# Dense and dilated-window attention with a gated sum: half the input by transposing DMAs, bound and query read-out re-ordered, planner settings changed

## The chip, the cores and the metric

The kernel runs on one core of a Trainium2 chip. The metric is device microseconds of one execution; the median of three runs before the change is 895.62 us (894.89 to 896.11).

The core has five engines with a queue of their own: TensorE (PE, matmuls; its weight loads are listed as PEld), VectorE (DVE), ScalarE (ACT), GpSimd (POOL) and SyncE (SP, here only a queue of DMAs). ACT and POOL issue DMAs too. Engines wait for each other by semaphores, and each works through its own list in order.

## The reference

Two attentions over the same input x (2048 x 640, bfloat16), with 32 heads of width 20, are mixed by a gate for each row.

```python
g = sigmoid((x * gate_w).sum(-1, keepdims=True))
# A: dense attention
q, k, v = split(x @ A_wqkv)             # (32 heads, 2048, 20)
p = softmax(q @ k.T * 20 ** -0.5)       # 2048 x 2048 for each head
a = merge(p @ v) @ A_wo
# B: eight keys for each row, at distance 0, 2, ..., 14 behind it
logits = where(idx >= 0, (q_B * k_B[idx]).sum(-1) * 20 ** -0.5, -1e9)
b = merge((softmax(logits)[..., None] * v_B[idx]).sum(w)) @ B_wo
out = g * a + (1 - g) * b
```

## The kernel before, in words

**Tiles.** The 32 heads of A are taken in eight quads of four; each head of a quad has 32 partitions (one for a bias, 20 for values), so that a quad fills 128. Queries are taken in four chunks of 512. A group is one chunk of one quad: 16 key blocks of 128 times four heads, 64 score units of 128 x 512. There are 32 groups and 2048 units. `GO` (line 37) is the order of the groups. Before, chunks 0 and 1 alternate for quads 0 to 3, then chunk 0 takes quads 4 to 7, then chunk 1; chunks 2 and 3 follow, all quads each.

**A step.** `mk_qk` (line 1233) puts the scores of three or two units into PSUM banks, in turns (banks 0 to 2, banks 3 and 4); `mk_exp` (line 1253, the instruction on line 1256) reads them with one exponential on ACT into one of six buffers `ebuf`. `mk_pv` (line 1267) multiplies the buffers with the values and sums in bank 5. When a group is closed, `gen_norm` (line 707) transposes, divides by the sum and multiplies by the gate on DVE.

**The bound.** Instead of a row's maximum, a bound on it is subtracted: the keys' largest absolute value in each channel (`k_max`, line 482, four pieces for a quad, and `mk_KM`, line 487) times the queries' absolute values (`q_abs`, `q_fin`, lines 658 to 668). One matmul adds the negative bound to a spare row of the projected query in its bank, and DVE reads the bank out as `qT`.

**Exponentials on DVE.** Some units go to DVE instead of ACT: `gen_xm` (line 1355) takes a free bank (6 or 7) or, by `xstep` (line 1331), the third bank of a step, and has the score matmul done; `gen_x` (line 1406) computes two units as a pair, in integer and polynomial steps, on lines 1424 to 1448. `X0` is the first step at which a unit may start, `XMIN` and `XLAST` are how many units a group (the last group) must have left, and 64 - `XAHEAD` is that number for the group after the current one.

**The planner.** The whole order is worked out when the kernel is built. Each piece of other work is a lane, a generator that says on which engine its next instruction runs and for how long. The main loop (line 1785) keeps a clock for each engine; before each step it fills PE's time until the step's banks come free with value matmuls, lanes, and spare matmuls (`spare`, line 1706, which write nothing that is read and run only while PE's share of work is under `SPW`). The lanes are: `gen_v`, `gen_k`, `gen_q` (projections of A), `gen_late` (weights of B and the output weights), `gen_F` (projections and logits of B for one chunk), `gen_K` (values, softmax and weighted sum of B), `gen_fold` (output projection of a chunk) and `gen_prefold` (the last chunk's in part). Their starts are steps (`gstep`, `FSTART`), and k, v and q lanes have due steps (`open_group`, line 1588). While a due step is less than six steps away, no new DVE unit starts (`urgent`, line 1298); `behind` and `hot` hold units back too, the first by a pace for the DVE work of the lanes (`LW`, `LS`). `GRP` is the least size of a batch of value matmuls.

**The start.** Lines 383 to 395 issue the loads: the first K weights on ACT's queue; x in eight tiles of 256 rows, the Q weights, the gate vector and the V weights on SP's. `pro_tr` (line 1103) transposes a tile by ten PE transposes, read out by DVE and ACT; `pro_k` (line 1127) projects the keys of quad 0 for it, DVE takes the largest value and ACT reads the keys out; `pro_q` (line 1147) projects the first query group in two halves. Lines 1163 to 1202 set their order by hand: a transpose, then the K projection of the tile before it. The bound, one group of values (read out by ACT) and `q_fin` close the start; then the main loop begins.

SP's queue carries, after that, the head weights of A (`ld_w`, line 434, five DMAs with runs of 40 bytes each), B's weights in blocks of 160 KB (`ldw`, line 884, in `gen_F`; three buffers) and the stores.

## Time and profile before

| | |
|---|---|
| median of three runs | 895.62 us |
| the profiled execution | 894.33 us, span 892.5 us |
| first exponential starts | 18.18 us |
| exponentials on ACT | 777, 1902 units |
| units on DVE | 146 |
| last exponential ends | 883.17 us |
| granted TensorE clock | 0.999 |

How to read it: times are from the start of the span, which is 1.8 us shorter than the execution's own time. A row names line, engine, operation, the tile written and the tiles read, shapes, count, busy time, mean duration, and the idle time of the engine just before, with the instruction that ended it. "ps" is PSUM. Instructions on one engine overlap a little, so that their mean duration is more than the distance from start to start. The DMA queue of an engine is its name with a q. Rows of x take 1280 bytes, the B weight blocks have rows of 256 bytes.

### The profile page before, as it was taken

What the parts mean: (1) busy time and instruction counts of PE and PEld (TensorE: products, weight loads), DVE (VectorE), ACT (ScalarE), POOL (GpSimd) and SP (SyncE); (2) the same over time, 40 slices, a digit from 0 to 9 for tenths busy, and PEclk for the clock granted to TensorE, in tenths of its full rate; (3) what the DMA queues carried; (4) which work ended last, traced back from release to release, by engine and by line L of the source; (5) the groups of instructions that cost most, each with busy time, mean ns of one, the idle gap of its engine ahead of it and who ended that gap; (6) DMA issues with size and microseconds to landing.
All of it is one profiled execution on the core that took longest, in us unless ns stands there. A gap on an engine that the chain in (4) does not pass through costs nothing.

```text
span 892.5 us, 15877 instructions
## 1 busy us (share of the span) xinstructions
PE 820.1 (92%) x6560; PEld 255.5 (29%) x6560; DVE 811.9 (91%) x1170; ACT 876.2 (98%) x804; POOL 87.8 (10%) x103
## 2 busy tenths in 40 slices
PE   9989999999999998999998889999988999888986
PEld 6322322223323222223332222233222232222322
DVE  6598889999998999999899999999999899999994
ACT  6999999999999999999999999999999999999996
POOL 1000000000000011220002222001322002222000
PEclk9999999999999999999999999999999999999999
DMA  8122101011011456572115658113847003865000
GB/s 181 41 49 48 21 9 10 1 28 7 4 11 14 86 93 94 90 123 37 17 19 88 111 102 145 25 16 56 143 78 108 10 10 74 131 93 89 2 1 30
DMA packets 140988, 51.26 MB, mean 57 GB/s; under 512 B 120436, under 2 KB 128628, under 8 KB 140916
## 3 DMA queue, kind: packets, MB, share of 16 engines
q0 software_dynamic: 13824, 31.46, 20.5%
q1 hardware_dynamic: 126164, 18.35, 13.4%
q8 instruction: 52, 0.85, 0.4%
q10 hardware_dynamic: 928, 0.43, 0.2%
q14 instruction: 20, 0.16, 0.1%
HBM read 16.14 MB, written 2.62 MB: 21 GB/s over the span
## 4 chain that ended last, share of the span: by engine, by line
ACT 94%; PE 2%; DMA 2%; DVE 1%; issue 0%; POOL 0%; DVEq 0%
ACT ebuf L1256 93%; DMA accW<-tmps 1%; PE ps L1112 1%; DMA accW<-xT 1%; PE ps L1136 1%; ACT L_sb L1004 0%; PE ps L411 0%; PE ps L1241 0%; DVE tmps L1069 0%; DVE accW L1059 0%; DVE qk L905 0%; ACT WvB L841 0%; PE ps L565 0%; DVE xH L1436 0%; PE ps L1153 0%
## 5 line engine op out<-in xcount | busy, mean ns | idle before, releaser
L1256 ACT ACTIVATE ebuf<-ps 128x1024 bf16<-128x1024 f32 (+1 forms) x777 | 862.7, 1485 | 0.9 <-PE ps L1241 0.8
L1241 PE MATMUL ps<-qT,kT 32*128 32x512 bf16 x1941 | 305.6, 384 | 63.9 <-ACT ebuf L1256 55.1
L1281 PE MATMUL ps<-ebuf,vA 128*21 128x512 bf16 x1902 | 182.6, 383 | 0.5 <-ACT ebuf L1256 0.5
L1241 PEld LDWEIGHTS ps<-qT,kT 32*128 32x128 bf16 x1941 | 74.3, 91 | 351.7 <-ACT ebuf L1256 327.2
L1424 DVE TENSOR_SCALAR xI<-ps 128x512 int32<-128x512 f32 x146 | 99.4, 686 | 28.3 <-PE ps L1396 14.8
L1436 DVE SCALAR_TENSOR_TENSOR xH<-xU 128x1024 f32<-128x1024 f32 x73 | 88.9, 1218 | 1.4
L1071 POOL DMA_DIRECT2D accW<-tmps x36 | 32.0, 987 | 586.2 <-DVE tmps L1069 545.8
L1439 DVE SCALAR_TENSOR_TENSOR xH<-xH,xU 128x1024 f32<-128x1024 f32 x73 | 88.7, 1216 | 1.0
L1448 DVE SCALAR_TENSOR_TENSOR xo<-xI,xH 128x1024 int16<-128x1024 int32 x73 | 88.7, 1215 | 0.6
L463 PE MATMUL ps<-xT,WqkB 128*128 128x512 bf16 x200 | 59.9, 383 | 0.0
L1281 PEld LDWEIGHTS ps<-ebuf,vA 128*21 128x21 bf16 x1902 | 35.8, 90 | 64.6 <-issue 56.7
L942 DVE TENSOR_TENSOR prod<-qk 128x1024 bf16<-128x1024 bf16 x80 | 51.8, 681 | 0.3 <-PE ps L918 0.3
L1433 DVE TENSOR_SCALAR xU<-xI 128x1024 f32<-128x1024 uint16 x73 | 49.8, 682 | 0.6
L463 PE MATMUL ps<-xT,WqP 128*128 128x512 bf16 x155 | 46.7, 383 | 0.0
L463 PE MATMUL ps<-woA_r,oTn 128*128 128x320 bf16 x236 | 45.3, 301 | 0.0
L463 PE MATMUL ps<-xT,accW 128*128 128x512 bf16 x140 | 42.2, 383 | 0.0
L1717 PE MATMUL ps<-ident,zt 128*128 128x512 bf16 x119 | 40.8, 386 | 0.0
L1712 PE MATMUL ps<-xT,ident 128*128 128x512 bf16 x130 | 40.1, 384 | 0.6 <-DVE qk L905 0.6
L1396 PE MATMUL ps<-qT,kT 32*128 32x512 bf16 x107 | 38.9, 383 | 0.8 <-DVE kT L475 0.7
L1069 DVE TENSOR_TENSOR tmps<-vB,attnT 128x1280 f32<-128x1280 bf16 x24 | 35.5, 1478 | 1.4 <-DMA accW<-tmps 1.4
L1069 DVE TENSOR_TENSOR xT<-vB,attnT 128x1280 f32<-128x1280 bf16 x24 | 35.4, 1477 | 0.3 <-DMA xT<-xT 0.3
L463 PE MATMUL ps<-WvA,oBacc 128*128 128x320 bf16 x160 | 33.2, 302 | 0.1
(122 smaller groups left out, 730.1 us busy)
## 6 DMA issues: line engine op xcount, KB each, us to landing
accW<-tmps POOLq DMA_DIRECT2D x36, 320.0 KB, 4.2
accW<-xT POOLq DMA_DIRECT2D x24, 320.0 KB, 4.0
xT<-xT POOLq DMA_DIRECT2D x24, 320.0 KB, 4.6
WqkB<-in_B_wqkv_dram SPq DMA_DIRECT2D x40, 160.0 KB
xT<-tmps POOLq DMA_DIRECT2D x12, 320.0 KB, 3.8
WqP<-in_A_wqkv_dram SPq DMA_DIRECT2D x135, 20.0 KB
x_tm<-in_A_x_dram SPq DMA_DIRECT2D x8, 320.0 KB
out_dram<-outsb SPq DMA_DIRECT2D x24, 80.0 KB
```

The source lines that it names most:

```text
L463: ins = e.matmul(o, l, r, start=(k0 + k == 0), stop=(k0 + k == n - 1))
L942: t = T("dve", lambda e, r=r, q_ap=q_ap, k_ap=k_ap: e.tensor_tensor(prod[r][:, :, :], q_ap, k_ap, ALU.mult), reads=["qB", "kB"], writes=[( ...
L1069: T("dve", lambda e, vv=vv, av=av, m=m: e.tensor_tensor(tmp4[m], vv, av, ALU.mult), reads=["aT", "vB4"], writes=[("tmps", m)] + dead, cost ...
L1241: ins = e.matmul(bank[b0 + i], kT[32 * j:32 * j + 32, q, kb * P:(kb + 1) * P], qT[gi % NQT][32 * j:32 * j + 32, :], start=True, stop=True)
L1256: return T("act", lambda e: e.activation(ebuf[s % NEB][:, 0:512 * n], ps[:, b0 * 512:(b0 + n) * 512], ACTF.Exp, scale=LN2 / ONE), reads=[( ...
L1281: ins = e.matmul(bank[OB][32 * j:32 * j + DH + 1, :], vA[:, q, kb, VW * j:VW * j + DH + 1], ap, start=st, stop=sp)
L1424: r = T("dve", lambda e, b=b, i=i: e.tensor_scalar(xI[:, 512 * i:512 * i + 512].bitcast(I32), bank[b], XB, 0.0, op0=ALU.add, op1=ALU.max), ...
L1433: T("dve", lambda e: e.tensor_scalar(xU[:, :], xI[:, :].bitcast(U16)[:, 0:2048:2], XV[0], XV[1], op0=ALU.mult, op1=ALU.add), reads=[("xI", ...
L1436: T("dve", lambda e: e.scalar_tensor_tensor(xH[:, :], xU[:, :], XC[0], xU[:, :], ALU.add, ALU.mult), reads=["xU"], writes=["xH"], cost=1220)
L1439: T("dve", lambda e: e.scalar_tensor_tensor(xH[:, :], xH[:, :], XC[1], xU[:, :], ALU.add, ALU.mult), reads=["xU"], writes=["xH"], cost=1220)
L1448: t = T("dve", lambda e, r=r: e.scalar_tensor_tensor(xo[r][:, :].bitcast(I16), xI[:, :].bitcast(I32), XC[2], xH[:, :], ALU.mult, ALU.add), ...
L1717: T("pe", lambda e: e.matmul(bank[OB], zt[:, :], ones4, start=False, stop=False, skip_group_check=True), reads=["ident", "zt"], accum=[("o ...
```

## The change

The first four x tiles are loaded plainly, on ACT's queue, followed by the Q weights; the other four are written straight into `xT` by four transposing DMAs on SP's queue, from which the first Q weights are gone. Four tiles then need no PE transposes and no read-outs; their K projections wait for the DMA. The order of the start is written anew: a plain tile's transpose, its K projection and that of a transposed tile in turn; the query's two halves come before the last K projection, and the first group of values goes to the lane `gen_v` in the stream, where DVE reads it out.

`k_max` reads two key blocks of 512 at once. `q_fin` is two functions, and in `gen_q` the read-out is a step of its own that waits its turn on DVE. The memsets of `woA_r` go from DVE to POOL, and no longer wait two steps each. In `gen_F` the additional wait before a weight block (`told`) is gone. `GO` takes chunks in turns for quads 0 and 1 only. The rest are the planner's settings: starts, due steps, pace, the smallest batch, limits on units and on taking a bank, the place of the unit lane among the others, and PE's share up to which spare matmuls run. With `XI` = 0 its two new lines do nothing.

```diff
--- before.py
+++ after.py
@@ -34,7 +34,7 @@
 
-GO = [(c, q) for q in range(4) for c in range(2)] + [(c, q) for c in range(2) for q in range(4, NQUAD)] + [(c, q) for c in range(2, QCN) for q in range(NQUAD)]
+GO = [(c, q) for q in range(2) for c in range(2)] + [(c, q) for c in range(2) for q in range(2, NQUAD)] + [(c, q) for c in range(2, QCN) for q in range(NQUAD)]
 GI = {x: i for i, x in enumerate(GO)}
@@ -381,11 +381,13 @@
     T("act", lambda e: e.dma_start(WqkA[:, :, 80:160], wA_v[:, :, D:D + 80]), writes=[("WkA", 0)], dma=True)
-    for h in range(NH):
-        T("sp", lambda e, h=h: e.dma_start(x_tm[:, 2 * h:2 * h + 2, :], x_v[:, 2 * h:2 * h + 2, :]),
+    for h in range(4):
+        T("act", lambda e, h=h: e.dma_start(x_tm[:, 2 * h:2 * h + 2, :], x_v[:, 2 * h:2 * h + 2, :]),
           writes=[("x_tm", h)], dma=True)
-
-    T("sp", lambda e: e.dma_start(WqkA[:, :, 0:80], wA_v[:, :, 0:80]), writes=[("WqA", 0)], dma=True)
+    for h in range(4, NH):
+        T("sp", lambda e, h=h: e.dma_start_transpose(xT[:, h // 2, :, 256 * (h % 2):256 * (h % 2) + 256], A_x[0][256 * h:256 * h + 256, :]),
+          writes=[("xTt", h, 0)], dma=True)
+    T("act", lambda e: e.dma_start(WqkA[:, :, 0:80], wA_v[:, :, 0:80]), writes=[("WqA", 0)], dma=True)
 
@@ -479,16 +481,20 @@
 
+    KMC = 2
+
     def k_max(q, tcc):
-        T("dve", lambda e: e.tensor_reduce(Kmax[:, q % 2, tcc:tcc + 1], kT[:, q, tcc * 512:(tcc + 1) * 512], AX.X, ALU.max,
+        n = KMC
+        o = 4 if n == 4 else tcc // n
+        T("dve", lambda e: e.tensor_reduce(Kmax[:, q % 2, o:o + 1], kT[:, q, (tcc + 1 - n) * 512:(tcc + 1) * 512], AX.X, ALU.max,
                                            apply_absolute_value=True),
-          reads=[("kT", q, tcc)], writes=[("Kmax", q % 2, tcc)], cost=690)
+          reads=[("kT", q, tcc - i) for i in range(n)], writes=[("Kmax", q % 2, o)], cost=150.0 + 533.0 * n)
 
...
         if part == 0:
-            src = Kmax0[:, :] if q == 0 else Kmax[:, q % 2, 0:4]
+            src = Kmax0[:, :] if q == 0 else Kmax[:, q % 2, 0:4 // KMC]
             T("dve", lambda e: e.tensor_reduce(Kmax[:, q % 2, 4:5], src, AX.X, ALU.max),
-              reads=[("Kmax0", h) for h in range(NH)] if q == 0 else [("Kmax", q % 2, t) for t in range(4)],
+              reads=[("Kmax0", h) for h in range(NH)] if q == 0 else [("Kmax", q % 2, t) for t in range(4 // KMC)],
               writes=[("Kmax", q % 2, 4)], cost=160)
@@ -508,7 +514,7 @@
             free = [b for b in (6, 7) if not held[b]]
-            if free and (len(free) == 2 or forcing[0] or not xwant() or cur[0] is xl_[0]) and not (cur[0] is xl_[0] and not forcing[0] and clk["dve"] > clk["pe"] + 3000.0):
+            if free and (len(free) == 2 or forcing[0] or not xwant() or cur[0] is xl_[0]) and not (cur[0] is xl_[0] and not forcing[0] and clk["dve"] > clk["pe"] + 300.0):
                 b = min(free, key=lambda k: (only is not None and k != only, free_at[k]))
@@ -631,9 +637,10 @@
             give(b, k_evac(b, q, tcc))
-            yield ("dve", 690.0, 0.0)
-            k_max(q, tcc)
-        for part in (0, 1):
+            if tcc % KMC == KMC - 1:
+                yield ("dve", 150.0 + 533.0 * KMC, 0.0)
+                k_max(q, tcc)
+        for part in (0, 1) if KMC < 4 else (1,):
             yield ("dve", 300.0, 0.0)
@@ -651,7 +658,9 @@
         yield ("pe", MM, 1.0)
-        give(b, q_fin(b, gi, q))
+        q_bound(b, gi, q)
+        yield ("dve", 690.0, 0.0)
+        give(b, q_evac(b, gi))
 
@@ -661,8 +670,14 @@
     def q_fin(b, gi, q):
+        q_bound(b, gi, q)
+        return q_evac(b, gi)
+
+    def q_bound(b, gi, q):
         T("pe", lambda e: e.matmul(bank[b], KM[:, q, :], qabs_hi, start=False, stop=True, skip_group_check=True),
           reads=["qabs", ("KM", q)], accum=[("bk", b)], cost=MM)
+
+    def q_evac(b, gi):
         qmade.add(gi)
@@ -682,9 +697,7 @@
         for q in range(NQUAD):
-            yield ("dve", 330.0, 0.0)
-            T("dve", lambda e, q=q: e.memset(woA_r[:, q, :], 0.0), writes=[("woA_r", q, j) for j in range(4)], cost=330)
-            yield ("s", 2)
+            T("pool", lambda e, q=q: e.memset(woA_r[:, q, :].bitcast(FP32), 0.0), writes=[("woA_r", q, j) for j in range(4)], cost=900)
         for q in range(NQUAD):
@@ -879,7 +892,6 @@
         wld = {}
-        told = {}
 
@@ -894,11 +906,10 @@
                 ldw(wi + NWB - 1)
-                yield ("t", max(wld[wi][1].fin, told.get(wi, 0.0)))
+                yield after(wld[wi][1])
                 b = yield from take(True)
...
                 mms = [(bank[b], W[:, c, :], xT[:, tc, c, :]) for c in range(CN)]
-                told[wi + NWB - 1] = max(clk["sp"], clk["pe"]) + 5800.0
                 yield from chain(b, mms, [("WqkB", wld[wi][0]), ("xT", tc)])
@@ -1028,7 +1039,7 @@
 
-            T("pe", pe_tb, reads=["L", "ident"], writes=[("bk", b)], cost=700, mode="t")
+            T("pe", pe_tb, reads=["L", "ident"], writes=[("bk", b)], cost=700, mode="t", flow=430.0)
 
@@ -1124,9 +1135,11 @@
 
+    KO = (0, 4, 1, 5, 2, 6, 3, 7)
+
     def pro_k(h):
         t, o = divmod(h, 2)
-        b = 6 + o if h < NH - 1 else 1
+        b = 6 + KO.index(h) % 2 if h < NH - 1 else 1
         ap = bank[b][:, 0:256]
@@ -1136,7 +1149,7 @@
 
-        T("pe", fn, reads=w_keys("WkP", 0) + [("xTt", h, k) for k in range(2)], writes=[("bk", b)], cost=550)
+        T("pe", fn, reads=w_keys("WkP", 0) + [("xTt", h, k) for k in range(2 if h < 4 else 1)], writes=[("bk", b)], cost=550)
         r = T("dve", lambda e: e.tensor_reduce(Kmax0[:, h:h + 1], ap, AX.X, ALU.max, apply_absolute_value=True),
@@ -1161,37 +1174,32 @@
     pro_tr(0)
+    pro_k(0)
+    pro_k(4)
     pro_tr(1)
-    pro_k(0)
+    pro_k(1)
+    pro_k(5)
     pro_tr(2)
-    pro_k(1)
+    ld_wk(1)
+    ld_wq(1)
     pro_tr(3)
-    for h in range(4, NH - 1):
-        pro_k(h - 2)
-        pro_tr(h)
-        if h == 4:
-            ld_wk(1)
-            ld_wq(1)
-    pro_tr(NH - 1)
-    for h in range(NH - 3, NH):
-        pro_k(h)
-        if h == NH - 3:
-            mk_q0()
+    pro_k(2)
+    pro_k(6)
+    mk_q0()
+    pro_k(3)
+    pro_q(0)
+    pro_q(1)
+    pro_k(7)
     mk_KM(0, 0)
     mk_KM(0, 1)
-    pro_q(0)
+    q_fin(QB0, 0, 0)
     T("dve", lambda e: e.tensor_copy(WvA[:, :, 1:2], gw[:, :].rearrange("p (c k) -> p c k", k=1)), reads=["gw", "WvA"],
       writes=["WvA"], cost=170)
-    pro_q(1)
     ld_wk(2)
...
     for t in range(QCN):
-        sch.bufs[("xT", t)] = [sch.bufs[("xTt", 2 * t + 1, 1)][0], []]
-    for i_ in range(3):
-        v_chunk(3, 0, 0, i_, i_)
-    v_evac(3, 0, 0, "act")
-    q_fin(QB0, 0, 0)
+        sch.bufs[("xT", t)] = [sch.bufs[("xTt", 2 * t + 1, 1 if t < 2 else 0)][0], []]
 
@@ -1310,10 +1318,10 @@
 
-    XAHEAD = 20
+    XAHEAD = 36
     XMIN = 28
-    X0 = 25
-    XLAST = 20
+    X0 = 18
+    XLAST = 16
 
@@ -1350,6 +1358,7 @@
     xres = {}
+    XI = 0
     XBO = 0
@@ -1432,9 +1441,13 @@
               reads=[("xI", 0), ("xI", 1)], writes=["xU"], cost=690)
+            if XI == 2 and not behind():
+                xidle[0] = True
             yield ("dve", 1220.0, 0.0)
...
               reads=["xU"], writes=["xH"], cost=1220)
+            if XI == 1 and not behind():
+                xidle[0] = True
             yield ("dve", 1220.0, 0.0)
@@ -1455,7 +1468,7 @@
 
-    LW, LS = 300000.0, (20, 700)
+    LW, LS = 315000.0, (20, 720)
     lwork = [0.0]
@@ -1571,11 +1584,11 @@
     kl, vl, ql, foldl = {}, {}, {}, {}
-    vl[0] = lane(gen_v(0, 1), "v0", 0)
+    vl[0] = lane(gen_v(0, 0), "v0", 0)
     lane(gen_late(), "late", 0)
-    FSTART = (1.0, 5.0, 9.0, 13.0)
+    FSTART = (1.0, 8.0, 14.0, 20.0)
     for tc in range(4):
-        lane(gen_K(tc), "K%d" % tc, gstep(5.0))
+        lane(gen_K(tc), "K%d" % tc, gstep(0.0))
         if tc < 3:
@@ -1583,7 +1596,7 @@
     started = set()
-    GRP = 10
+    GRP = 8
 
@@ -1593,15 +1606,15 @@
         ql[ng] = lane(gen_q(ng), "q%d" % ng, s + 2, 0)
-        ql[ng].dl = s + 24
+        ql[ng].dl = s + 18
         for k in range(1, NQUAD):
...
                 kl[k] = lane(gen_k(k), "k%d" % k, s, 0)
-                kl[k].dl = int(FU[k] * GST) - 0
+                kl[k].dl = int(FU[k] * GST) - 12
         for p in range(1, NQUAD // 2):
...
                 vl[p] = lane(gen_v(p), "v%d" % p, s + 2, 0)
-                vl[p].dl = int(FU[2 * p] * GST) + 6
+                vl[p].dl = int(FU[2 * p] * GST) + 0
 
@@ -1698,7 +1711,7 @@
     spares = [0]
-    SPW = .65
+    SPW = .7
     zsp = [0]
@@ -1743,7 +1756,7 @@
             return [xlane, xmlane] + act
-        if xlane.hold and 1:
+        if xlane.hold and 0:
             n = sum(1 for g in act if g.hold or (g.name[:4] == "norm" and int(g.name[4:]) not in obrd))
...
         return act + [xmlane, xlane]
```

## The prediction

> **What bounds the kernel now.** I read the table of busy engines first: ScalarE (ACT) is busy for 98% of the span, TensorE (PE) and VectorE (DVE) for over 90% each, so the first question is which of the three may not wait.
>
> ```profile
> PE 820.1 (92%) x6560; PEld 255.5 (29%) x6560; DVE 811.9 (91%) x1170; ACT 876.2 (98%) x804; POOL 87.8 (10%) x103
> ```
>
> Then the chain that ended last, as shares, and the ACT groups with their forms kept apart. Ninety-three hundredths of the chain are the exponentials of line 1256, and before them ACT sat idle for 0.9 us in 777 instructions. PE and DVE are late nowhere in a way that stops ACT.
>
> ```profile
> ACT 94%; PE 2%; DMA 2%; DVE 1%; issue 0%; POOL 0%; DVEq 0%
> ...
> L1256 ACT ACTIVATE ebuf<-ps 128x1536 bf16<-128x1536 f32 x349 | 599.5, 1718 | 0.9 <-PE ps L1241 0.8
> L1256 ACT ACTIVATE ebuf<-ps 128x1024 bf16<-128x1024 f32 x427 | 523.0, 1296 | 0.0
> ```
>
> Third, the chain in order of time, in its first 40 us: columns are start, length, what. The reader is to see that the first exponential starts at 18.18, and that what leads up to it is PE work without a hole.
>
> ```profile
> 12.56 1.74 PE ps L1136 x15
> 14.29 1.09 PE ps L1153 x10
> 15.39 0.03 issue
> 15.41 1.23 PE ps L565 x15
> 16.65 0.24 PE ps L664
> 16.89 0.02 issue
> 16.91 0.70 DVE qT L667
> 17.61 0.14 issue
> 17.75 0.41 PE ps L1241 x3
> 18.16 0.02 issue
> 18.18 21.79 ACT ebuf L1256 x19
> ```
>
> The last exponential ends at 883.17 (ACT's timeline: a run from 858.74 for 24.43 us), and a serial tail of 9.3 us follows (normalize, four matmuls, add, store). So the span is a start of 18.18, a gapless ACT stream of 865.0, and a tail of 9.3; a change counts only by one of these. The stream is set by how many of the 2048 score units DVE takes from ACT. The DVE groups give that price:
>
> ```profile
> L1424 DVE TENSOR_SCALAR xI<-ps 128x512 int32<-128x512 f32 x146 | 99.4, 686 | 28.3 <-PE ps L1396 14.8 <-PE ps L1241 10.4 <-PE ps L463 0.7
> L1436 DVE SCALAR_TENSOR_TENSOR xH<-xU 128x1024 f32<-128x1024 f32 x73 | 88.9, 1218 | 1.4
> ...
> L483 DVE TENSOR_REDUCE Kmax<-kT 128x1 f32<-128x512 bf16 x28 | 18.7, 670 | 0.2
> ...
> L686 DVE MEMSET woA_r<- 128x320 uint32 x8 | 2.6, 325 | 0.1
> ```
>
> 146 units went to DVE, in pairs of 2x686 + 682 + 1218 + 1216 + 1215 = 5703 ns, so 2.85 us of DVE a unit. A unit is worth 1718 - 1296 = 422 ns of ACT (the two forms of line 1256). Ten us of DVE made free are thus 1.5 us of time. DVE has some to give: windows from 18.18 to 876.90 add up to 795.4 busy in 858.7, so 63 us idle, of which 12.3 lie before 38.2, while PE is full with projections.
>
> **The change part by part.** *Input.* Four of eight x tiles lose 10 PE transposes each (0.56 us in the chain) and two evacuations. The plain tiles move to ACT's DMA queue behind the first weight load, so the first is issued at about 1.25 instead of 0.74. WqA goes with them. I put each of ACT's five added issues at 0.49, as its own at 0.75; the table load of ACT then ends near 5.1, and the first ACT evacuation was at 5.29. SP issues four transposing DMAs in place of eight loads and WqA, then gw, WvA and the weight loads, in that order. Eight issues took 4.27, so nothing later slips unless one transposing issue takes over 1.2.
>
> The transposing rate is in no row. From 4 to 10 the plain rows of 1280 bytes came at 363 GB/s; a load of 256-byte rows (WqkB) ran at 248 at 51 to 52; the 40-byte runs of the head weights gave 29 at 14 to 15. A transposing read of 128 columns is 256 bytes, so I take 248, with 363 and 29 as ends. Starting at 2.3, 0.2 MB of weights and 1.31 MB plain at 363 and 1.31 MB transposed at 248 are all in at 2.3 + 4.2 + 5.3 = 11.8.
>
> The Trainium skill, DMA: Bandwidth & Descriptors, section Latency and other measured facts, has 261 GB/s for one kernel's transposing DMA. By that figure the sum would be the same within 0.3 us; no run here shows it.
>
> The new order, by the same rows: first transposes at 4.8 (0.5 for the issue, 0.3 for sharing the engines), 0.56 each; a K projection 0.55; between a transpose's end and its K projection 0.85 (evacuation 0.60, and 0.25 of waits around it, as at 5.2 to 6.06). Tr0 ends 5.36; k0 and k4 6.2 to 7.3; tr1 to 7.87; k1 and k5 8.7 to 9.8; tr2, tr3 to 10.95; k2, k6, k3 to 12.9; two query halves to 14.0; k7 to 14.5. Holes of 1.9 us eat most of the 2.24 saved. From the end of k7 the old rows are 1.0 to the finished bound (14.29 to 15.28), 0.53 to the read-out, 1.27 to the exponential: first exponential at 17.3. Tr3 waits for the last plain tile a little if the data end at 11.8, so I take 17.6: **-0.6**, between -1.2 (first tile 0.6 sooner) and +0.6 (k7's data at 15.4).
>
> *The first V group* (15 matmuls, 1.23; ACT 0.57 + 0.17) goes from the start into the stream. It was behind the query's abs read-out (15.42 to 16.11), so on the path it cost only 0.3 (bound matmul at 16.48), counted above. It now costs DVE 0.65 + 0.15 and PE 1.23 in a stretch where PE is 95% full; its cover is the six exp buffers, 6 x 1.11 us, before a value matmul has to come.
>
> *DVE work.* Eight memsets of 325 go to POOL: 2.6 free. POOL has only the vA memset before them (512 elements in 2.46), at 4.8 ns an element at most 12.3 us in all, and no DMA of POOL's queue is due before 300; SP's wo loads, which wait for them, come at 74. Line 483 goes from 28 reduces of 512 to 14 of 1024; by the slope to line 1140 (425 for 256) one takes about 1160, so 18.7 becomes 16.2: 2.5 free, between 0 (twice the price) and 9 (the same price). Later by one tile, the bound has slack, as it is due groups later. Together 2.6 + 2.5 - 0.8 = 4.3 us of DVE: 1.5 units.
>
> *Order.* Units may start at step 18, not 25: DVE is at 7.32 of 7.80 there already, nothing. The last pair may start with 16 units left, not 20: the last ended at 876.85, 6.3 before the stream's end, and a pair takes 5.7: it may just fit, 2 units. Of the 50 us that DVE idles after 38.2 (28.3 at line 1424, waiting for a score matmul) I give a tenth to the new limits on taking a bank and to units taken further ahead: 5 us, 1.75 units; ends -8 and +8 units, as nothing in the trace prices an order. Sum of units: 1.5 + 2 + 1.75, so +5, **-2.1 us**; ends are 8 fewer in all (+3.4) and 1.5 + 2 + 8 more, with 2 beside if the reduces are cheap (-5.7).
>
> *Query read-out by turns, W loads without the extra wait, flow.* Splitting the bound from the read-out lets other DVE work in between; 32 times, 0 on ACT as long as a query is a group early. It puts the read-out behind at most one instruction (1.2). The W loads of branch B landed within 3.7 us of issue (48.5 to 52.2), under the 5.8 that the plan assumes, so the dropped wait costs nothing. Spare matmuls at a share of 0.70 fill PE holes only; the granted clock is 1.00 in every window of the stream. Where no stall goes from ACT's path, none is late next but the fold of a chunk, which the planner forces before the chunk after the next one closes its first group.
>
> **Sum:** 894.33 - 0.6 - 2.1 = 891.6 for an execution like the profiled one (span 892.5, 1.8 around it). That one lies 1.3 under the median of 895.62, so on the median 892.9, 0.3% faster. Differences under 0.2% (1.8 us) can't be told from none with this kernel.
>
> **Rivals.** *Slower, by the order.* The groups now go one chunk at a time from group 4 on, so quad 3 is due at group 5, not 6, and quad 7 at group 9 (261 us at 27.0 a group), not 11 (315). Six K quads at 5.3 of DVE, three V pairs at 3.6, and their queries fall into 189 us instead of 243, with due times 12 and 6 steps sooner, and units stop whenever one is within 6 steps. For it: from 200 to 300 there are 16 units only, against 20 in 700 to 800. Against: DVE work put earlier makes room later. If the stops make DVE idle by 23 us more, 8 units are lost: +3.4 - 0.6, 898.4. From 1.4 lost units the start's gain is gone; from 6 it is slower by more than can be told from no change.
>
> *Slower, transposing data late.* k7 needs the last tile by 14.0. At 100 GB/s the data end at 2.3 + 4.2 + 13.1 = 19.6, the first exponential is at 19.6 + 0.55 + 2.8 = 23.0, and the stream's gain of 2.1 is overrun by 2.7: 898.3. At 125 GB/s the two cancel. For it: 256-byte rows already lose a third. Against: the need is spread, a tile each 2.5 us. PE holes of this sort would also bare ACT's start.
>
> *Much slower, block by block.* If the transposes go as slowly as the 40-byte runs, 1.31 MB at 29 GB/s take 45 us; the first exponential is near 53, at 928. The Trainium skill, VectorE: DVE Perf Modes, section The three transpose paths, gives 1309 ns for one 128x128 block by DMA against 390 by TensorE; forty in a row would be an estimate of 52 us. No run here shows which; that page's own remark on the fast path speaks against it.
>
> *No change.* Holes after each transpose and the late first tile take back the start, the last pair doesn't fit, and only the 1.5 units of freed DVE are left: -0.6 us, 895.0.
>
> **How the numbers follow.** Forecast (faster) 0.50; no change 0.17; the order 0.18; late data 0.12; block by block 0.03. So faster 0.50, same 0.17, slower 0.33. The forecast's own range is 889.5 (start -1.2, 8 units more, a little beyond) to 893.8. The whole range, 889.5 to 900.0, leaves out block by block, a third each of the two slower cases, and some 0.07 below.
>
> **What would show it.** Right: first exponential near 17.6, with K projections never waiting for a DMA; about 151 units on line 1424's successor; ACT idle before the exponentials under 2 us; tail 9.3; reduces of 1024 near 1160. Wrong: PE idle in the start with a DMA as releaser; under 146 units; ACT waiting for score matmuls in 70 to 260; a last pair that ends after the stream.

## The result, and the profile after

The changed kernel takes 906.31 us (median of four executions, 905.02 to 907.55) against 895.8 before: a ratio of 1.0119, interval 1.0101 to 1.0136. It is 1.2% slower; the forecast was 0.3% faster. The profiled execution is the 907.55 one, with a span of 905.7, so the profiles differ by 13.2 us where the medians differ by 10.5.

| us | before | after |
|---|---|---|
| first exponential starts | 18.18 | 24.58 |
| from there to the end of the last | 864.98 | 872.08 |
| ACT idle in that stretch, gaps over 0.15 | 0 | 4.83 |
| tail | 9.34 | 9.04 |
| units on DVE, exponentials on ACT | 146, 777 | 144, 789 |

The start gave 6.4 us of the 13.2 and idle time of ACT 4.8. The other 2.0 go with 2 units more on ACT (2 x 422 ns = 0.8), 12 more exponentials, and 0.3 less in the tail.

TensorE's timeline of the changed kernel (start, length, instructions, count; in brackets the idle time before and its releaser):

```profile
6.51 0.73 PE L1123 MATMUL ps<-ident,x_tm 128*128 128x128 bf16 x10 [2.35 <-DMA x_tm<-in_A_x_dram]
9.02 2.29 PE L1149 MATMUL ps<-xT,accW 128*128 128x256 bf16 x10 [1.77 <-ACT xT L1132]
11.10 1.27 PE L1123 MATMUL ps<-ident,x_tm 128*128 128x128 bf16 x10
13.15 2.29 PE L1149 MATMUL ps<-xT,accW 128*128 128x256 bf16 x10 [0.78 <-ACT xT L1132]
...
19.43 0.72 PE L1149 MATMUL ps<-xT,accW 128*128 128x256 bf16 x5 [0.48 <-ACT kT L1155]
19.98 1.25 PE L1166 MATMUL ps<-xT,WqP 128*128 128x256 bf16 x10
21.07 0.71 PE L1149 MATMUL ps<-xT,accW 128*128 128x256 bf16 x5
22.87 0.40 PE L677 MATMUL ps<-qabs,KM 128*128 128x512 bf16 x1 [1.09 <-DVE KM L500]
```

The reader is to see four things. The first tile is there at 6.51, where it was at 4.01; after it nothing on TensorE in the start waits for a DMA. The first two pairs of K projections wait for the read-out of a transpose that has just run. While TensorE has such holes, its work is slow: 2.29 for a pair of K projections, which takes 1.25 in a run below that fills the holes. And between the last K projection and the bound's matmul lies a wait of 1.09 for DVE, where the old kernel had the query projections. SP's timeline shows why everything on its queue came late:

```profile
0.74 12.42 SPq L388 DMA_TRANSPOSE xT<-in_A_x_dram  x4
...
13.85 0.51 SPq L397 DMA_DIRECT2D WvA<-in_A_wqkv_dram  x1
...
25.39 0.51 SPq L689 DMA_DIRECT2D qk<-in_B_wqkv_dram  x1
```

Four transposing issues hold SP for 12.42 us, 3.1 each (1.4 to 5.0). The V weights are issued at 13.85, before at 6.73; branch B's load into `qk` at 25.39, before at 20.25. An instruction on DVE waits for that last one. First DVE's timeline, then TensorE's, then ACT's:

```profile
30.39 0.09 DVE L973 MEMSET vB<- 128x35 uint32 x1 [5.07 <-DMA qk<-in_B_wqkv_dram]
30.43 0.66 DVE L589 CAST vA<-ps 128x480 bf16<-128x480 f32 x1
31.01 0.15 DVE L598 COPY zg<-ps 128x3 f32<-128x3 f32 x1
```

```profile
31.21 1.01 PE L571 MATMUL ps<-WvA,xT 128*128 128x161 bf16 x9 [1.93 <-DVE zg L598]
```

```profile
24.58 2.37 ACT L1264 ACTIVATE ebuf<-ps 128x1536 bf16<-128x1536 f32 x2 [1.71 <-PE ps L1249]
28.18 2.37 ACT L1264 ACTIVATE ebuf<-ps 128x1536 bf16<-128x1536 f32 x2 [1.24 <-PE ps L1249]
32.95 2.52 ACT L1264 ACTIVATE ebuf<-ps 128x1536 bf16<-128x1536 f32 x2 [2.40 <-PE ps L1249]
35.80 4.62 ACT L1264 ACTIVATE ebuf<-ps 128x1536 bf16<-128x1536 f32 x4 [0.33 <-PE ps L1249]
```

A memset of 88 ns, the first instruction of `gen_K`, waits 5.07 us. It clears the margin of `vB4`, and `qk`, a different buffer, is what the DMA fills; but both took over the memory of `x_tm`, so the kernel's list of readers and writers puts one behind the other. Before, `gen_K` began at `gstep(5.0)` and the load had long landed; now it begins at `gstep(0.0)`. Behind the memset stands the read-out of the first V group, moved from ACT in the start to DVE in the stream. TensorE's next V matmuls wait for that bank, the next scores stand behind them in TensorE's list, and ACT runs dry at 32.95. The stall of 1.24 before it, at 28.18, is another: TensorE had V and query matmuls ahead of the scores, 15 of the V matmuls in 2.08 us where the old kernel takes 1.23.

The exponentials themselves and the DVE work that the forecast counted, by forms:

```profile
L1264 ACT ACTIVATE ebuf<-ps 128x1536 bf16<-128x1536 f32 x326 | 554.2, 1700 | 5.7 <-PE ps L1249 5.7
L1264 ACT ACTIVATE ebuf<-ps 128x1024 bf16<-128x1024 f32 x463 | 541.2, 1281 | 0.9 <-PE ps L1249 0.9
```

```profile
L1433 DVE TENSOR_SCALAR xI<-ps 128x512 int32<-128x512 f32 x144 | 98.0, 685 | 37.8 <-PE ps L1249 20.5 <-PE ps L1405 15.7 <-DVE xo L1461 0.5
L489 DVE TENSOR_REDUCE Kmax<-kT 128x1 f32<-128x1024 bf16 x14 | 16.9, 1208 | 0.2
```

DVE is busy for 803.3 us, 8.6 less than before. But its units idle 37.8 before their first instruction, 9.5 more than before: the freed time was not turned into units.

### The profile page after: what moved, and what is told of

It reads as the page before. It is cut to its first block, busy times and chain, and to the rows that moved or that the text cites. A ratio compares the mean times of both kernels' runs of the same rounds, so it can differ in the third digit from the quotient of the medians.

```text
span 905.7 us, 15987 instructions
## 1 busy us (share of the span) xinstructions
PE 845.8 (93%) x6598; PEld 262.3 (29%) x6598; DVE 803.3 (89%) x1140; ACT 876.0 (97%) x810; POOL 89.2 (10%) x111
## 4 chain that ended last, share of the span: by engine, by line
ACT 94%; PE 3%; DVE 2%; issue 1%; DMA 1%; ACTq 0%; DVEq 0%
ACT ebuf L1264 93%; DVE WvB L696 1%; PE ps L1149 1%; DMA x_tm<-in_A_x_dram 1%; ACT L_sb L1015 0%; PE ps L1249 0%; PE ps L465 0%; PE ps L1123 0%; PE ps L1289 0%; PE ps L571 0%; DVE vA L589 0%; ACT WvB L854 0%; DVE xI L1433 0%; ACT L405 0%; PE ps L1166 0%
## 5 line engine op out<-in xcount | busy, mean ns | idle before, releaser
L1249 PE MATMUL ps<-qT,kT 32*128 32x512 bf16 x1972 | 310.8, 386 | 42.8 <-ACT ebuf L1264 33.5
L1289 PE MATMUL ps<-ebuf,vA 128*21 128x512 bf16 x1904 | 186.1, 385 | 0.0
L1433 DVE TENSOR_SCALAR xI<-ps 128x512 int32<-128x512 f32 x144 | 98.0, 685 | 37.8 <-PE ps L1249 20.5
L1725 PE MATMUL ps<-xT,ident 128*128 128x512 bf16 x186 | 56.7, 384 | 0.3 <-DVE xI L1433 0.3
L1730 PE MATMUL ps<-ident,zt 128*128 128x512 bf16 x145 | 46.6, 384 | 0.0
L571 PE MATMUL ps<-WvA,xT 128*128 128x160 bf16 (+1 forms) x320 | 31.8, 241 | 1.9 <-DVE zg L598 1.9
```

The source lines that it names most:

```text
L1249: ins = e.matmul(bank[b0 + i], kT[32 * j:32 * j + 32, q, kb * P:(kb + 1) * P], qT[gi % NQT][32 * j:32 * j + 32, :], start=True, stop=True)
L1289: ins = e.matmul(bank[OB][32 * j:32 * j + DH + 1, :], vA[:, q, kb, VW * j:VW * j + DH + 1], ap, start=st, stop=sp)
L1433: r = T("dve", lambda e, b=b, i=i: e.tensor_scalar(xI[:, 512 * i:512 * i + 512].bitcast(I32), bank[b], XB, 0.0, op0=ALU.add, op1=ALU.max), ...
L1725: T("pe", lambda e, b=b: e.matmul(bank[b], ident[:, :], xT[:, 3, 0, :], start=True, stop=True), reads=["ident", ("xT", 3)], accum=[("bk", ...
```

## The experiments

Theory after the result: the loss is the start plus the memset's wait. Rival: the order and its settings lose it in the stream. Ratios are to the kernel before, run on the same chip.

**One part at a time, planned anew.** The first four change one part and let the planner work out the order.

```diff
# e1_old_start: the changed kernel; loads, transposes and first V group as before
# e2_new_start_only: the kernel before; loads and order of the start as changed, first V group in the stream
# e3_K_later: the changed kernel
-        lane(gen_K(tc), "K%d" % tc, gstep(0.0))
+        lane(gen_K(tc), "K%d" % tc, gstep(5.0))
# e4_old_start_K_later: e1 and e3 together
```

> The changed kernel with the start of the kernel before: all x tiles by plain loads on SP's queue and PE transposes, old order, first V group in the start. Theory 'start' (the loss lies in the input and the order of the start: first exponential at 24.58 instead of 18.18, and a half-clock PE behind it): first exponential back at 18.2, PE clock 1.00 throughout, 897 to 899 us; what is left above 895.8 is the DVE wait of the early value lane for branch B's weights (5.07 us in the changed kernel) and the order. Rival 'order' (the new planner order loses by itself): stays at 903 or above.

> The kernel before with only the new start: transposing DMAs for half of x, plain half on ACT's queue, new order of the start, first V group in the stream. Theory 'start': first exponential near 24.6, one or two stalls of ACT in the first 15 us of the stream, 903 to 905 us. Rival 'order': under 898 us.

> The changed kernel with the lanes for branch B's values starting at step 128 as before, not at step 0. Theory 'early value lane': the DVE wait of 5.07 us for the weight DMA at 25 to 30 us goes, and with it ACT's stall of 2.40 us: 903 to 904 us. Rival 'half clock' (ACT's stalls after 24.6 come from PE at half clock alone): the stalls stay, 906 us within 1.

> The changed kernel with the old start and the value lanes at step 128: what is left of the change is the order and the settings, the paired maximum and the memsets on POOL. If these give the 2.1 us that the prediction put on them: 893.5 to 894. If they are neutral: 895 to 896.5. Rival 'order loses': 897.5 or more, with fewer than 146 units on DVE.

| | us | ratio, interval | first exp. | ACT idle after | tail |
|---|---|---|---|---|---|
| e1_old_start | 924.79 | 1.0321 [1.0295, 1.0347] | 18.38 | 15.8 | 20.71 |
| e2_new_start_only | 935.77 | 1.0442 [1.0423, 1.0461] | 24.34 | 8.96 | 34.04 |
| e3_K_later | 912.35 | 1.0188 [1.0167, 1.0209] | 25.11 | 5.06 | 9.63 |
| e4_old_start_K_later | 914.55 | 1.0222 [1.0182, 1.0261] | 18.21 | 5.2 | 17.39 |

All four are slower than both kernels, even the two whose first exponential is back at 18.2 to 18.4. The planner starts from the clocks at the end of the start, so any edit there gives another order for all of the 2048 units: tails of up to 34 us, 136 to 146 units on DVE. None of the times that I expected for the theories came true; the rivals of e1 and e4 did by number, and p6 below decides on them. The four show where the first exponential comes from and price nothing else. From here on the stream is held: the clocks handed to the planner are set to those of the original, and the stream then has the same instructions in the same order.

**The start and the wait, with the changed kernel's stream.**

```diff
# p1_pinned_old_start: loads and order of the start as before; first V group and stream as changed
# p5_no_dve_wait: the changed kernel, memset without the wait for the load into qk
-            T("dve", lambda e: e.memset(vB4[:, :, 0:PADB], 0.0), ...)
+            m_ = T("dve", lambda e: e.memset(vB4[:, :, 0:PADB], 0.0), ...)
+            m_.deps = [d for d in m_.deps if d.dom != "dma"] + xrd_   # xrd_: the readers of x_tm
# p6_old_start_no_wait: both
```

> The changed kernel's stream, instruction for instruction (the planner's clocks at the end of the start are set to those of the changed kernel), behind the old start without its V group: all x plain on SP's queue, eight PE transposes in the old order. Theory 'start' (6.4 us before the first exponential, and the half-clock PE behind it): first exponential at 18, PE clock 1.00 from 18 to 38, ACT idle in the stream only by the DVE wait for the weights of B (2.4 to 4 us): 898 to 901 us. Rival 'order' (the stream's new order is what loses): the stream from first to last exponential stays at 872, and the total is 900 only by the earlier start; then 865 for the old order leaves 7 us for the order.

> The changed kernel with one wait less: the memset of branch B's value halo, early in the stream, no longer waits for the weight DMA, whose target is other memory; every instruction and its place stay. Theory 'early value lane': DVE's 5.07 us of idle at 25 to 30 go, ACT's stall of 2.40 at 32.95 goes or shrinks under 0.8: 903 to 904. Rival 'half clock': PE is still at 0.50 from 25 on and ACT stalls by as much: 906 within 0.8.

> The changed kernel's stream behind the old start without its V group, and without the DVE wait for B's weights: what is left of the change is the order, the paired maximum, the memsets on POOL and the V group in the stream. Theory 'the rest is neutral or a little worse' (144 units on DVE instead of 146, 789 steps instead of 777): first exponential at 18.0, ACT idle in the stream under 1 us, 896 to 898 us. Rival 'the order gains what was predicted for it': 894 or less. Rival 'the order loses by itself': over 899.

| | us | ratio, interval | first exp. | ACT idle after |
|---|---|---|---|---|
| p1_pinned_old_start | 903.50 | 1.0094 [1.0069, 1.0118] | 18.04 | 6.13 |
| p5_no_dve_wait | 903.43 | 1.0084 [1.0059, 1.0109] | 25.57 | 1.09 |
| p6_old_start_no_wait | 896.05 | 1.0006 [0.9998, 1.0015] | 18.39 | 0.45 |

ACT's timeline of the run with both (its exponential is line 1280):

```profile
18.39 22.70 ACT L1280 ACTIVATE ebuf<-ps 128x1536 bf16<-128x1536 f32 x20 [2.55 <-PE ps L1265]
```

The exponentials start near the old time and run without a gap. With the new group order, the new settings, 14 reduces for 28, the memsets on POOL and the read-out by turns all in it, the time can't be told from the kernel before. So the rival falls: the order is neither the loss nor a gain. Start and wait together cost 906.31 - 896.05 = 10.3 of the 10.5 us. How the 10.3 divide depends on which is undone first. With the wait gone, the start costs 903.43 - 896.05 = 7.4 and the wait is left 906.31 - 903.43 = 2.9. With the start undone alone (p1, which I had expected at 898 to 901) only 2.8 come back: the memset then waits longer, 6.5 us, and taking that wait away gives 903.50 - 896.05 = 7.4. In p1 the load into `qk` was issued at 20.00, no later than in the old kernel. So it is the early start of `gen_K` that makes the wait, with or without transposing DMAs ahead of the load. The intervals leave each of the single shares open by 2 to 3 us.

**What in the start.** Four runs take one suspect each.

```diff
# c1_fills: the changed kernel with 38 more matmuls on zeros in the holes of the start
+    fill(10)   # and 7, 4, 4, 4, 2, 5 further on; two more in pe_fill
# c2_plain_bytes: the changed kernel, same bytes and rows, without transposing;
#   half of x is then in the wrong order
-        T("sp", lambda e, h=h: e.dma_start_transpose(xT[...], A_x[0][256 * h:256 * h + 256, :]), ...)
+        T("sp", lambda e, h=h: e.dma_start(xT[...], bass.AP(tensor=A_x.tensor, ...)), ...)
# p8_no_wait_act_sems: p5, and
-    DMA_POOL = {"sp": 16, "act": 4, "pool": 12}
+    DMA_POOL = {"sp": 16, "act": 8, "pool": 12}
# p10_no_wait_act_sems_fills: p8 with the fills of c1
```

> The changed kernel, same stream, with 38 matmuls on zeros put into PE's waits in the start, so that PE is not idle there. Theory 'half clock': granted clock 1.00 instead of 0.50 from 8 to 18 and from 25 to 28; K projections 0.55 again instead of 1.1; first exponential at 20 to 21 instead of 24.6; 900 to 902 us. Rival 'landing' (the start waits for data, PE's clock is hidden behind it): first exponential within 1 us of 24.6.

> The changed kernel with the four transposing DMAs replaced by plain ones that write the same bytes to the same places untransposed, so that half of x is in the wrong order in what is computed. It prices the transposition alone. Theory 'transposing issue': SP's four issues take 2 us instead of 12.4, the first plain tile lands at 5 instead of 6.5, the weights behind them are issued by 5 instead of 13.9, first exponential at 18.5 to 19.5: 898 to 900 us. Rival 'sharing' (two queues at once are what delays the tiles, whatever they carry): first tile still at 6.5 and first exponential over 22.

> The changed kernel without the DVE wait, and with eight DMA semaphores for ACT's queue instead of four, so that ACT's sixth load (WqA) no longer waits for the first x tile to land before ACT can go on to its table load. Theory 'ACT held by its own queue': table load before 5.5 instead of near 7 to 9, first K projection 0.9 to 1.1 after the first transposes instead of 1.8, first exponential 1 us earlier than with the wait, 902 to 902.6 us against 903.4. Rival: the first tile's landing alone sets it, 903.4 within 0.7.

> As the run with eight semaphores and without the DVE wait, and with the 38 matmuls on zeros in the start. With the DVE wait gone an earlier start can no longer be lost at it. Theory 'half clock': first exponential 1 us earlier again, granted clock 1.00 from 0 to 38, no stall of ACT in the stream, 900.5 to 901.5 us. Rival 'landing': as without the fills, 902.3 within 0.7.

| | us | ratio, interval | first exp. | ACT idle after |
|---|---|---|---|---|
| c1_fills | 912.35 | 1.0188 [1.0167, 1.0208] | 23.57 | 11.04 |
| c2_plain_bytes | 905.90 | 1.0114 [1.0094, 1.0135] | 22.24 | 4.95 |
| p8_no_wait_act_sems | 903.57 | 1.0083 [1.0067, 1.0099] | 23.01 | 0.33 |
| p10_no_wait_act_sems_fills | 904.08 | 1.0089 [1.0077, 1.0101] | 22.94 | 1.92 |

SP's timeline of the run with plain bytes:

```profile
0.74 2.97 SPq L388 DMA_DIRECT2D xT<-in_A_x_dram  x4
```

The issues cost 12.42 us because they transpose: plain ones of the same bytes take 2.97. Without transposing the first exponential comes 2.3 us sooner. Of that 0.7 is there at the first transpose (5.85 against 6.51); most of the rest is TensorE's pace, as the second pair of K projections takes 1.25 there and not 2.29. That is not the plain DMAs' doing alone: p2, which transposes, has 1.25 for it too. The first exponential is still 4.1 later than before, and as the memset's wait is still there the time hardly moves. The fills made K pairs take 1.25 and the first exponential 1.0 us earlier; the stream then lost more, since the memset waited 7.3 us. With the wait gone, fills did not lower the time (904.08 against 903.57). Eight semaphores let ACT's table load start at 4.16 instead of 6.89, where it had waited for an x tile to land to have a semaphore back, and the time did not fall either (903.57 against 903.43). All four times missed what I expected for the theory. p8's rival came true, and half of c2's (first exponential over 22, but the first tile not at 6.5).

A gain of a microsecond or two from either can't be excluded. The intervals of p5, p8 and p10 are 1.1 to 2.2 us to either side, and a first exponential is that of one execution: the same start gave 24.58, 25.11 (e3) and 25.57 (p5). What the four runs do show is that these suspects are not the bulk: with the slow matmuls filled up, ACT's queue freed and the wait gone, p10 still takes 8.5 us more than the kernel before. The first four tiles' landing and the chain behind it are what is left.

**Queues and order, with the old kernel's stream.** Here the old kernel is the base, its stream held.

```diff
# p2_before_new_start: the kernel before with the changed start, first V group kept there
# s1_two_queues: the kernel before, all plain, old order, eight semaphores for ACT;
#   the first query weights on ACT's queue too, behind the four tiles
-        T("sp", lambda e, h=h: e.dma_start(x_tm[...], x_v[...]),
+        T("act" if h < 4 else "sp", lambda e, h=h: e.dma_start(x_tm[...], x_v[...]),
# s3_plain_first: p2, but one queue for x, and gw, WqA, WvA on ACT's queue, eight semaphores
-        T("act", lambda e, h=h: e.dma_start(x_tm[...], x_v[...]),
+        T("sp", lambda e, h=h: e.dma_start(x_tm[...], x_v[...]),
```

> The kernel before, its stream instruction for instruction, behind the new start (transposing DMAs, plain half on ACT's queue, new order), with the first V group kept in the start ahead of the bound's matmul. The value lane of B starts at step 128 here, so that no DVE wait for B's weights stands in the stream. Theory 'start costs what it delays': first exponential at 24.5 to 25.5, stream 865 to 866 without stalls of ACT, 902 to 903 us. Rival 'the stream hides it' (a late start is partly given back): under 900.

> The kernel before, its stream kept instruction for instruction, with one edit in the start: x's tiles 0 to 3 are loaded by ACT's queue and tiles 4 to 7 by SP's, all eight plain and all eight transposed by TensorE in the old order; ACT has eight DMA semaphores, so that none of its issues waits. Theory 'landing' (tiles that come by two queues at a time share the DMA engines, so the first of them lands later, and everything hangs on the first four): the first tile is transposed at 5.0 to 6.0 us where the kernel before had 4.0, the first exponential is at 19.5 to 21, and the time is 897 to 898.5. Rival 'order' (what costs in the changed kernel is the serial order of transposes and K projections and the slow transposing issues, not the sharing): first exponential at 18.2 within 0.4, time 895.6 within 0.8.

> The kernel before, its stream kept, with the changed kernel's start except for the queues: SP issues plain tiles 0 to 3 first and the four transposing DMAs behind them, and gw, the first query weights and the V weights' first half go by ACT's queue with eight semaphores. So the first tile meets no other transfer of x. Theory 'landing': the first tile is transposed near 4.0 and the first four K projections come early, but the four transposing issues (12.4 us for four in the changed kernel) then begin near 2.5 and end near 15, so the last tile lands near 17 and the first exponential is at 20 to 22: 897.5 to 899.5. Rival 'order' (the new order of the start costs by itself): first exponential at 23 or later, as with the changed kernel's start (24.06 with the same stream), and 901 or more. Rival 'the first tile alone': first exponential at 18 to 19 and the time of the kernel before, 895.6 within 1.

| | us | ratio, interval | first exp. | ACT idle after |
|---|---|---|---|---|
| p2_before_new_start | 904.19 | 1.0095 [1.0082, 1.0108] | 24.06 | 2.91 |
| s1_two_queues | 900.67 | 1.0055 [1.0043, 1.0068] | 23.05 | 1.23 |
| s3_plain_first | 911.27 | 1.0169 [1.0155, 1.0184] | 30.15 | 2.56 |

With the old stream, and with nothing held up at a memset, the new start costs 8.5 us (p2; I had expected 902 to 903). So the rival, that the stream hides a late start, falls. TensorE's timeline of the run with two plain queues:

```profile
6.29 1.25 PE L1111 MATMUL ps<-ident,x_tm 128*128 128x128 bf16 x10 [2.13 <-DMA x_tm<-in_A_x_dram]
8.62 1.25 PE L1111 MATMUL ps<-ident,x_tm 128*128 128x128 bf16 x10 [1.08 <-DMA x_tm<-in_A_x_dram]
9.66 1.28 PE L1135 MATMUL ps<-xT,accW 128*128 128x256 bf16 x5
10.72 1.27 PE L1111 MATMUL ps<-ident,x_tm 128*128 128x128 bf16 x10
11.79 1.04 PE L1135 MATMUL ps<-xT,accW 128*128 128x256 bf16 x5
```

Nothing is transposed by DMA here and the order is the old one; only the first four tiles, and the query weights behind them, come over ACT's queue. That alone makes the first transpose 2.3 us late, the first K projection 3.6 (9.66 against 6.11) and the first exponential 4.9, and costs 4.9 us of time (900.67 against 895.72), more than I had expected. Of the 4.9, 2.3 are the first tile and 1.1 the wait for the second. The rest is lost by 12.7: until then ten transposes take 1.25 and a K projection 1.28 and 1.04, where the old kernel needed 0.72 and 0.71 from 6.7 on.

One queue brings the tiles one after the other in the order of need. Here tile 0 stands on ACT's queue behind the K weights (0.10 MB), and tile 4 has its old place at the head of SP's. By 3.5 us SP's queue had moved 0.33 MB, one whole tile, and ACT's 0.08 MB, not yet all of the K weights; in the old kernel SP's 0.33 MB by then were tile 0. So tile 0 started late. How much of that is the K weights ahead of it and how much the other queue beside it, no run separates. The Trainium skill, DMA: Bandwidth & Descriptors, section Issuing engines are not separate DMA queues, says that DMAs from all engines run on the same 16 engines and interleave, so that a second issuer saves only issue time. This trace agrees in that the second queue brought the first tile no sooner: 6.29 against 4.01.

In the third run the plain tiles are alone at first. TensorE's and SP's timelines:

```profile
4.12 1.13 PE L1114 MATMUL ps<-ident,x_tm 128*128 128x128 bf16 x10
6.02 0.71 PE L1140 MATMUL ps<-xT,accW 128*128 128x256 bf16 x5 [0.78 <-ACT xT L1123]
14.86 1.25 PE L1140 MATMUL ps<-xT,accW 128*128 128x256 bf16 x5 [8.13 <-DMA xT<-in_A_x_dram]
```

```profile
2.79 14.10 SPq L388 DMA_TRANSPOSE xT<-in_A_x_dram  x4
```

The first tile is back at 4.12, but the order wants a transposed tile for its second projection, and that one was in only at 14.86, 12.1 us after its issue began (0.8 MB of V weights on ACT's queue went beside it). I had expected the last tile to decide, near 17; it was the first. By number the rival "order" came true, but by this wait. So this order wants the transposing DMAs at the head of SP's queue, and then the plain tiles have to go by the other queue, where the first came at 6.51.

**Fewer transposing DMAs.** Three starts for the kernel before, x on SP's queue alone, the last tiles transposed by DMA.

```diff
# b1_two_transposed: x tiles 0 to 5 plain, 6 and 7 by transposing DMAs right behind them,
#   WqA on ACT's queue, pro_q(0), pro_q(1) ahead of pro_k(6), pro_k(7)
# b2_two_after_weights: WqA, gw, WvA on SP ahead of the two; q, k(5), q, k(6), k(7)
# b3_one_transposed: as b2, only tile 7; k(5), q, k(6), q, k(7)
# all three: eight semaphores for ACT
```

> The kernel before, its stream kept, with six tiles of x loaded plain on SP's queue and transposed by TensorE in the old order, and only the last two brought in transposed by two DMAs on SP behind them; the query projections stand ahead of the last two K projections; the first query weights go by ACT's queue. Theory 'landing': two transposing issues take about 6 us where four took 12.4, so the last tile is in near 11 to 12.5, before its K projection could begin in any case, and two transposes with their read-outs (some 0.6 us of TensorE each in the kernel before) go: first exponential at 16.8 to 17.6, time 894.3 to 895.2. Rival (a transposing issue holds later loads of SP's queue, the V weights among them, and the gain is lost in the stream): first exponential as said, but ACT idle in the stream by 1 us or more, 896 or above.

> As the run with two transposed tiles, but SP issues the six plain tiles, the query weights, gw and the first half of the V weights before the two transposing DMAs, so that the V weights no longer wait for them, and the query projections stand between the last K projections. Theory 'landing': the V projections' wait for DVE's gate fold (1.35 us there) goes; the two transposing issues run from some 6 to 12 us, the last tile lands near 14, and its K projection, that could begin at 13.5, waits 0.5 or so: first exponential 17.6 to 18.4, time within 0.6 of 895.6. Rival (SP's later weight loads, now behind 6 us of transposing issues, come too late for the stream): first exponential the same, ACT idle in the stream over 1 us, 896.5 or above.

> The same with seven plain tiles and one transposing DMA, issued behind the V weights. Theory 'landing': one issue of 3 us from near 6.8 to 9.8, the tile in by 12, its K projection not before 13, so it is hidden; one tile's transposes (0.64 us of TensorE) go: first exponential 17.4 to 18.0, time 895.0 to 895.6. Rival (SP's later loads late): as for two tiles, but half as much: 896 to 896.5.

| | us | ratio, interval | first exp. | SP's transposing issues |
|---|---|---|---|---|
| b1_two_transposed | 897.34 | 1.0016 [1.0007, 1.0025] | 19.59 | 6.08 for two |
| b2_two_after_weights | 900.15 | 1.0046 [1.0032, 1.0059] | 20.83 | 6.21 for two |
| b3_one_transposed | 898.35 | 1.0042 [1.0024, 1.0059] | 19.53 | 2.76 for one |

All three missed my numbers, and none beats the kernel before. TensorE's timeline of the run with one transposed tile:

```profile
14.91 0.72 PE L1139 MATMUL ps<-xT,accW 128*128 128x256 bf16 x5
16.76 1.23 PE L568 MATMUL ps<-WvA,xT 128*128 128x161 bf16 x15 [1.12 <-DVE WvA L1188]
```

No projection waits for a transposed tile in it, and yet the first exponential is 1.35 later. The V weights had long been issued (5.40); the wait of 1.12 is for DVE, which after the last K projection has its maximum to take and the bound to make before it folds the gate into the V weights. The old kernel runs the query projections in that time, as its chain shows (14.29 to 15.38). Moved ahead of the last K projection they leave the wait bare; so it was in the changed kernel (1.09), and in p2 (1.17). That the order alone, without any transposing DMA, costs this much was not run by itself.

## Why the prediction was wrong, point by point

- *Input, the failed step.* I took -0.6, with +0.6 as the worse end; it was +6.4. The term that failed first is the arrival of the first tile, "first transposes at 4.8 (0.5 for the issue, 0.3 for sharing the engines)". They came at 6.51, and at 6.29 in s1, where nothing is transposed by DMA: the 0.8 was 2.3 to 2.5. By s1 the move of the first four tiles to ACT's queue costs 4.9 us of the kernel's time. I priced total bytes over total rate, which is right for when all are in, and not for when the first is in.
- *The transposing issue.* The text set its own condition, "nothing later slips unless one transposing issue takes over 1.2": one takes 3.1. The price of an issue that no row showed was tacitly that of a plain one, and the bound from both sides that I gave the rate was never given to the issue. What the late queue behind it cost is not shown by itself: c2, with 2.97 for 12.42, took 905.90.
- *ACT's queue.* I put the end of its table load near 5.1; the last of its six loads waited for a tile's landing, and the table load ended at 8.17. p8 shows no cost of this that can be told from none.
- *Order of the start.* "Holes of 1.9 us" were 1.77 and 0.78 at the first two pairs and 0.48 at the projection of tile 3, 3.0 in all, and I let "from the end of k7 the old rows" hold although the query projections that filled that stretch had moved: +1.1.
- *First V group.* Its cover, "the six exp buffers", was the wrong one. What ended it was not a full buffer: TensorE's list stood at a V matmul whose bank DVE had not read. And I did not cost the new start of `gen_K` at all, whose memset held DVE. Undoing its wait gave 2.9 us behind the new start and 7.4 behind the old.
- *DVE work.* The reduce measured 1208 (I said 1160), the eight memsets 2.85 us on POOL (I said at most 12.3). Sizes right; the gain didn't come, as DVE's units idled 9.5 longer, and 10.2 longer in p6 with the old start.
- *Order of the stream.* +5 units were forecast, 2 fewer came, and p6 shows the sum of order and settings as nothing: 896.05. My rival "slower, by the order" did not happen either: after 36 us ACT idles for 0.9 in all.
- *The last pair* ended at 892.85, 3.8 before the stream's end. It fitted, as said.
- *Rivals.* "Transposing data late" had the right sign (TensorE idle with a DMA as releaser) and 898.3. That its sign came is luck: the late tiles were the plain ones, and no K projection in the changed kernel's trace waited for a transposing DMA. Block by block fell.

What stays open: what makes the first tile late in s1, the K weights ahead of it or the other queue; how the 3.6 us that p2 loses beyond s1 (8.5 against 4.9) split between transposing, the holes of the order and the bare 1.1 us; and how much TensorE's slow pace in the start costs.

## What to carry to other kernels

Before the half of a load that is wanted first moves to a second queue, ask what stands ahead of it there and what takes its old place; here the first tile came 2.3 us later and the kernel took 4.9 more. When two delays lie one behind the other, undoing either alone shows little: here 2.8 and 2.9 us, and 10.3 for both. Before work is moved ahead of or behind a serial chain, ask which wait it was filling. And when a lane is started earlier, look at what its first instruction waits for: 88 ns of memset held three engines.

## What the runs showed of the hardware

A transposing DMA of 256 x 640 values held SP's queue for 2.76 to 3.5 us, on average over a run's issues, in the runs shown here, a plain one of the same bytes 0.74 (c2) and the plain x tiles 0.50 to 0.58 (before, after, s1 and s3); I had let the plain price stand for both.

TensorE's windows of the changed kernel give the granted clock (the figure after the POOL column):

```profile
0.00:18.00 18.00, 12.10 (x70) 7.97 (x71) 6.42 (x27) 5.45 (x10) 5.49 (x15) 0.72 1.04 198
18.00:38.00 20.00, 16.06 (x117) 8.26 (x115) 7.59 (x21) 11.52 (x13) 0.00 (x0) 0.83 0.65 102
```

The old kernel had 1.00 in both stretches; I had argued from that. But this figure does not tell how fast TensorE works in the start. p5 has the same start; a window and a line of its TensorE timeline:

```profile
8.00:18.00 10.00, 7.96 (x55) 6.21 (x53) 3.37 (x7) 4.76 (x9) 0.00 (x0) 1.00 1.16 178
```

```profile
9.83 2.29 PE L1155 MATMUL ps<-xT,accW 128*128 128x256 bf16 x10 [1.26 <-ACT xT L1138]
```

The figure is 1.00, and a pair of K projections takes 2.29, as in the changed kernel, which has 0.50 in that window. The old kernel, at 1.00, needs 2.27 for its first twenty transposes and 0.72 for each later ten. So the durations have to be read. By them, work in a start with holes takes up to 1.8 times as long, and with the holes filled (c1) the pair takes 1.25: a wait also makes the work behind it slower. How long that lasts differs between executions of the same order: the second pair took 1.25 in p2 and 2.29 in p5. The Trainium skill, TensorE: Matmul & The Clock Gate, section What's actually happening, has the half rate as the state after an idle stretch. The durations here agree (2.29 against 1.25 for a pair). What it cost this kernel is open: filling the holes did not lower the time (p10 904.08, p8 903.57).
